# Reordering the start of a recurrent-attention and expert kernel: score copies, early loads and group preparation take other places in the queues

## The chip, the cores and the metric

One core of a Trainium2 chip runs the whole program. The metric is device time in microseconds, from the start to the end of one execution. A second number, the span, runs from the first to the last instruction that the profiler recorded on the core; the profiled execution has both. The engines are TensorE (PE; PEld is its weight load), VectorE (DVE), ScalarE (ACT), GpSimd (POOL) and SyncE (SP, which here only issues DMAs; SPq is its queue). Every engine takes its instructions strictly in the order in which the program lists them.

## What is computed

The reference is a recurrent attention over 768 steps, for 4 x 8 heads of width 40, whose output goes through a top-2 mixture of 8 experts:

```python
for t in range(S):
    y[:, :, t] = np.einsum('bhd,bhde->bhe', rt, state)
    Sa = np.einsum('bhde,bhe->bhd', state, at)
    state_decay = state * wt[:, :, None, :] - np.einsum('bhd,bhe->bhde', Sa, bt)
    state = state_decay + np.einsum('bhd,bhe->bhde', vt, kt)
...
logits = x @ w_gate                    # x: the attention output, 3072 x 320
noisy_logits = logits + np.log1p(np.exp(x @ w_noise)) * noise
# top 2 experts of each row, softmax of their two logits
h = np.maximum(x[mask] @ w1[e], 0.0)
out[mask] += top2_w[mask, k, None] * (h @ w2[e])
```

## The kernel before, in words

The attention is computed in chunks of 64 steps. The 4 batches are two pairs (p = 0, 1) and the 12 chunks are six groups of two (g = 0 to 5), so that each group has four blocks and the loop in `run` goes over 24 blocks n (g = n // 4; inside a group the chunk changes every two blocks and the pair every block). What a block needs of its group is prepared beforehand:

- `loadA` (L528) loads w (`raww`, two buffers) and b and a (`rawba`, one buffer; for group 0's second pair two `X` buffers instead). `prepA` (L536) makes the running product of w with a scan on VectorE (`Gx`), its reciprocal with a logarithm and an exponential on ScalarE (L546, L547), four products on VectorE (L549 to L554), multiplies b and a, and splits each into two 16-bit halves with `pack` (L495): ScalarE makes one half (L500), VectorE the other (L501). Six DMAs from SyncE's queue then stack the halves into `st_ab` (L568).
- `scoresL` (L602) multiplies the stacks on TensorE (`score32`) and ScalarE copies each result into `X` and `lo` (L609).
- With both pairs' scores in `X`, `cover` (L613) masks them, `turn` (L614) transposes them in 32 x 32 squares on VectorE, `tsolve` (L617) inverts with 30 steps of two products (on VectorE for group 0, on GpSimd for groups 1 to 5), and `turn` transposes back. `prepM`, `prepT` and `prepU` in `run` call these for a group: the mask, the first `turn` with the inverse, and the second `turn`.
- `loadC` and `prepC` (L582, L586) load the keys (`rawk`, one buffer), multiply and pack them, and write them to DRAM (`d_k`), from where `fetchA` reads them back as `st_k`. `fetchA` and `fetchR` (L628, L638) also load `Vz`, `vu` and `RV` for a block.

A block n then runs `pre` (its key scores), `blocks`, `chain` (TensorE applies the inverse, in `pQ`, and VectorE writes the state `Sst`, L730, kept as `s.aD`), `outp` (the block's output) and the router's `logits`. Inside the loop a block prepares pieces of the group two ahead.

What sets the order: the program is written down in one sequence, and a planner in the build then simulates it and gives each engine the instruction that is ready first by its own cost estimates; the written order breaks ties. Three means bind it: `issue_after(ins)` (named `after` in `run`) puts what a block of code creates on the engine of `ins` behind `ins`, on that engine alone; `Behind(tc, eng, first)` does so for each instruction called through it, on the engine `eng`; `high_priority` moves work ahead among what is ready. None of the three makes an engine wait for data.

Instructions called through `Behind` are recorded under its line, L436, those of `burst` and the matmul helpers under L511 and L512.

Once attention is over, the eight experts are computed (`experts`), each by two large matrix products, the first waiting for weights that are loaded where attention's buffers were.

Of the kernel before, what the change touches and what calls it, by code (L numbers as in the profile page):

```python
# [8 lines left out]
F32 = mybir.dt.float32  # L9
# [33 lines left out]
class Moe:  # L43
# [70 lines left out]
    def turn(s):  # L114

        s.early=s.decode("0",1,4)
# [324 lines left out]
class Att:  # L441
# [53 lines left out]
    def pack(s,src,scl,h,nc_,out,V=None):  # L495

        nc=s.nc
        pk=s.tmp.tile([120,nc_*2,X//nc_],F16,name="pk",bufs=PKB)
        v=pk.rearrange("p (c l) x->p c l x",l=2); sv=src.rearrange("p (c x)->p c x",c=nc_)
        nc.scalar.activation(v[:,:,h],sv,AF.Copy,scale=scl)  # L500
        s.pd=(V or nc.vector).scalar_tensor_tensor(v[:,:,1-h],sv,scl,v[:,:,h],op0=ALU.mult,op1=ALU.subtract)  # L501
        out(pk)
# [83 lines left out]
    def prepC(s,G,gate=None,kf=None,first=None):  # L586
# [5 lines left out]
        if p==0 and g==0:  # L592
            s.mags=s.cp.tile([120,1],F32,name="mags")
            nc.vector.tensor_reduce(s.mags,kf[:,0:64],axis=AX.X,op=ALU.max)
        k_=kf.rearrange("p (c a b t)->p c a (b t)",c=CG,a=3,b=2)
# [17 lines left out]
    def cover(s,Xt,eng): eng.tensor_tensor(Xt,Xt,s.tri.to_broadcast([128,32,32]),op=ALU.mult)  # L613
    def turn(s,Xt):  # L614

        v=Xt.rearrange("p a b->p b a"); return s.nc.vector.transpose(v,v)
    def tsolve(s,Xt,eng):  # L617
# [114 lines left out]
    def outp(s,o,sD,xout):  # L732
# [19 lines left out]
        xout=xout[:,0:DM]  # L752
        xo=xout.rearrange("p (h e)->p h e",h=8); nc.vector.tensor_tensor(xo,Y[:,:,0:40],xo,op=ALU.mult)

    def run(s,m,xo=None):
# [3 lines left out]
        def prepA(g,p):  # L759
            if p==0: grp[g]=[]; scr[g]=s.tmp.tile([128,32,32],F32,name="X",bufs=3)  # L760
            with s.tc.high_priority(offset=PA_):
                G=s.prepA(p,g,rA.pop((g,p),None),first.get((g,p))); grp[g].append(G); s.scoresL(G,p,scr[g])
        E=lambda g: nc.gpsimd if g in TPOOL else nc.vector
        def prepM(g): s.cover(scr[g],E(g) if g>1 else nc.vector)
        def prepT(g):
          with s.tc.high_priority(offset=PT_ if g else BURST):
            s.xd=s.turn(scr[g]); s.tsolve(scr[g],E(g))
        def prepU(g):
          with s.tc.high_priority(offset=PT_ if g else BURST):
            s.turn(scr[g]); scr2[g]=scr[g]  # L770
        def prepC(g,p): s.prepC(grp[g][p])
# [12 lines left out]
        rA[0,0]=s.loadA(0,0); rA[0,1]=s.loadA(1,0); kf=s.loadC({'p':0,'g':0})  # L784
        prepA(0,0); prepA(0,1); s.consts1()
        s.prepC(grp[0][0],kf=kf,first=s.pd); fA(0); fR(0)
        s.prepC(grp[0][1],first=s.pd); fA(1); fR(1)
        prepM(0); prepT(0); tl0=s.tl; tl=tl0.ins
        s.pre(O[0],s.tm); s.blocks(O[0])
        prepU(0)  # L790
        for n in range(4): fB(n)
        first[1,0]=first[1,1]=tl0
        prepA(1,0); prepA(1,1); prepM(1); prepT(1)
        if m is not None:
            with after(tl): m.consts2(s.dm.bitcast(F32))
        xts=[]; aD=tl0
        for n in range(N):
# [3 lines left out]
            if q%2==0 and gn<NG:  # L801
# [3 lines left out]
                grp[gn].append(s.prepA(q//2,gn,rA.pop((gn,q//2)),aD))  # L805
            if n<2: s.prepC(grp[1][n],first=tl0)
            elif q%2==0 and gn<NG:
                with behind(n-1): rC[gn,q//2]=s.loadC(grp[gn][q//2])
# [9 lines left out]
            aD=s.aD  # L818
            if q==2 and w+1<NG:
                prepU(w+1)  # L820
                for t in range(4): fB(4*w+4+t)
            if n+1<N: s.pre(O[n+1])
            if q==3 and gn<NG: prepT(gn)
            xt=s.wk.tile([128,360],F32,name="xt",bufs=2)
            s.outp(O[n],sD,xt); xt=xt[:,0:DM]
# [163 lines left out]
```

## Time and profile before

| what | value |
|---|---|
| timed runs, median of 3 | 975.82 us (973.9 to 977.76) |
| profiled execution | 969.27 us |
| its span | 967.4 us |
| busy in the span: PE, DVE, ACT, POOL | 763.3, 595.3, 382.3, 366.4 us |
| first use of an inverse by TensorE | 76.80 us |
| attention ends, experts follow | about 536 us |

A row of the timeline gives the start and the duration in us, the engine, the line, the operation, what it writes and reads with the shapes, how often it stands there in a row, and in brackets the idle time of the engine before it and what ended that. A DMA's row is its issue, not its landing. A row of the table by stretch gives for each engine the busy time and the number of instructions, then the granted TensorE clock as a share of its full rate, the DMA engines' busy share and GB/s. Averages over the span hide that its start, its loop and the experts have different limits, so the rows below are taken by stretch.

### The profile page before, as it was taken

The numbers are of one execution on the slowest core, as the hardware profiler recorded it, in microseconds if no ns is written. First come the engines' busy times: TensorE is split into PE (matmuls) and PEld (weight loads), VectorE is DVE, ScalarE is ACT, GpSimd is POOL, SyncE is SP. The second block draws the span as 40 slices with busy tenths as digits, with TensorE's granted clock in tenths as the row PEclk, the third lists the DMA queues.
The fourth block names the chain that finished last, engine by engine and source line by source line (L and its number), as shares of the span: only waits on it lengthen the run. The fifth ranks groups of instructions, "written<-read, shape, count | busy, mean of one in ns | idle before, by whom it ended". The sixth has DMA issues, their size and how long they took to land.

```text
span 967.4 us, 32608 instructions
## 1 busy us (share of the span) xinstructions
PE 763.3 (79%) x14248; PEld 675.4 (70%) x14248; DVE 595.3 (62%) x1295; ACT 382.3 (40%) x787; POOL 366.4 (38%) x516
## 2 busy tenths in 40 slices
PE   0115546898886878887999579899999999999994
PEld 0114435777775766766777478889899999998994
DVE  6499673767888697537657672673637372737340
ACT  3204342644533455333454432443434343434320
POOL 6000087087188049429300205224243525252312
PEclk9995557987977999888999799899999999999997
DMA  9524555475572645543331714556556656664412
GB/s 227 168 73 122 159 157 137 126 178 143 144 201 67 161 134 149 161 125 126 89 104 42 232 49 71 85 168 85 171 84 183 105 157 119 145 130 125 55 16 35
DMA packets 99507, 121.09 MB, mean 125 GB/s; under 512 B 37832, under 2 KB 83596, under 8 KB 99276
## 3 DMA queue, kind: packets, MB, share of 16 engines
q1 hardware_dynamic: 89244, 101.87, 39.9%
q0 software_dynamic: 10112, 17.05, 10.5%
q8 instruction: 114, 1.87, 0.9%
q14 instruction: 37, 0.30, 0.1%
HBM read 76.69 MB, written 24.74 MB: 105 GB/s over the span
## 4 chain that ended last, share of the span: by engine, by line
PE 48%; DVE 7%; POOL 4%; issue 3%; ACT 2%; another core or an unknown queue 2%; DMA 1%; SPq 0%; POOLq 0%; ACTq 0%
PE ph L303 18%; PE po L330 17%; PE psc L511 2%; POOL X L626 2%; POOL Tt L624 2%; PE pY L511 2%; PE pW L511 2%; PE pQ L511 1%; DMA w2r<-in_w_dram 1%; PE po L322 1%; PE po L320 1%; DVE ohB L165 1%; PE pst L511 1%; DVE ohA L163 1%
## 5 line engine op out<-in xcount | busy, mean ns | idle before, releaser
L333 POOL DMA_INDIRECT out_dram<-y,oi x56 | 88.7, 1583 | 203.7 <-ACT y L332 195.3
L303 PE MATMUL ph<-xT,w1h 128*128 128x256 f16 (+1 forms) x1280 | 141.8, 256 | 9.1 <-issue 4.9
L303 PEld LDWEIGHTS <-w1h 128*128 128x128 f16 x1280 | 110.4, 99 | 20.8 <-issue 12.3
L305 ACT ACTIVATE r<-ph 128x320 f32<-128x320 f32 (+1 forms) x128 | 65.4, 518 | 112.9 <-PE ph L303 66.1
L330 PEld LDWEIGHTS <-hh 128*128 128x128 f16 x1536 | 108.9, 98 | 0.8 <-issue 0.8
L626 POOL TENSOR_TENSOR X<-X,Tt 128x30 f32<-128x30 f32 (+9 forms) x150 | 96.3, 642 | 11.0
L303 PE MATMUL ph<-xT,w1l 128*128 128x256 f16 (+1 forms) x768 | 93.2, 256 | 6.2 <-issue 6.1
L624 POOL TENSOR_TENSOR Tt<-X 128x30 f32<-128x30 f32 (+9 forms) x150 | 92.4, 616 | 10.7
L241 DVE SCALAR_TENSOR_TENSOR w2l<-w2r,w2h 128x1280 f16<-128x1280 f32 x16 | 23.3, 1490 | 89.1 <-ACT w2h L240 88.0
L303 PEld LDWEIGHTS <-w1l 128*128 128x128 f16 x768 | 66.7, 99 | 12.9 <-issue 8.5
L307 DVE CAST hh<-r 128x320 f16<-128x320 f32 (+1 forms) x128 | 48.3, 378 | 44.2 <-ACT r L305 28.4
L259 POOL DMA_INDIRECT xr<-xd,gi x56 | 57.2, 1022 | 44.9 <-issue 14.3
L309 DVE TENSOR_TENSOR hl<-r,hh 128x256 f16<-128x256 f32 (+1 forms) x128 | 71.8, 561 | 3.9
L511 PE MATMUL psc<-RV,uT 128*64 128x128 f32 x384 | 61.7, 312 | 10.4 <-DVE P L743 7.0
L743 DVE TENSOR_TENSOR P<-psc,mk 128x512 f32<-128x512 f32 x48 | 33.0, 687 | 53.1 <-PE psc L511 53.0
L330 PE MATMUL po<-w2h,hh 128*128 128x160 f16 x768 | 62.2, 235 | 0.5 <-DVE tab L169 0.5
L511 PE MATMUL psc<-RV 128*64 128x128 f32 x384 | 61.7, 312 | 0.0
L511 PEld LDWEIGHTS psc<-RV,uT 128*64 128x64 f32 x384 | 48.3, 156 | 18.5 <-DVE P L743 9.3
L330 PE MATMUL po<-w2h,hl 128*128 128x160 f16 x768 | 61.1, 233 | 0.0
L330 PE MATMUL po<-w2l,hh 128*128 128x160 f16 x768 | 61.0, 233 | 0.0
L511 PEld LDWEIGHTS <-st_ab 120*32 120x32 f16 (+2 forms) x1312 | 26.7, 112 | 43.7 <-issue 38.5
L330 PEld LDWEIGHTS <-hl 128*128 128x128 f16 x768 | 54.7, 98 | 0.0
(321 smaller groups left out, 1577.0 us busy)
## 6 DMA issues: line engine op xcount, KB each, us to landing
st_ab<-pk SPq DMA_DIRECT2D x72, 180.0 KB
w2r<-in_w_dram SPq DMA_DIRECT2D x8, 1280.0 KB
RV<-in_rv_dram SPq DMA_DIRECT2D x48, 192.0 KB
w1r<-in_w_dram SPq DMA_DIRECT2D x8, 1024.0 KB
rawba<-in_fm_dram SPq DMA_DIRECT2D x22, 360.0 KB
raww<-in_fm_dram SPq DMA_DIRECT2D x12, 365.6 KB
rawk<-in_fm_dram SPq DMA_DIRECT2D x12, 360.0 KB
d_k<-pk SPq DMA_DIRECT2D x12, 360.0 KB
```

Of the source, the lines that this page charges most:

```text
L241: nc.vector.scalar_tensor_tensor(l,w,sc,o,op0=ALU.mult,op1=ALU.subtract,accum_out=s.wsum[:,s.nw:s.nw+1]); s.nw+=1
L259: k=t//128; s.held(nc.gpsimd.indirect_dma_start(out=X[:p,k if s.cap==CAP else 0],out_offset=None,in_=s.xd[int(w is not s.early[0])],in_off ...
L303: for a,b in cut(n): nc.tensor.matmul(ph[:,a:b],w[:,k,fs],X[:,j,t0+a:t0+b],start=i+a==0,stop=i==7,skip_group_check=True)
L305: g=nc.scalar.activation(r[:,:n],ph[:,:n],AF.Relu,scale=HSC/(XS*W1S))
L307: nc.vector.tensor_copy(hh[:,f,:n],r[:,:n])
L309: if c.stop>c.start: nc.vector.tensor_tensor(o,r[:,c],hh[:,f,c],op=ALU.subtract)
L330: for a,b in cut(DM): s.lm=nc.tensor.matmul(po[:p,a:b],h[:,f,r],w[:,f,a:b],start=k+a==0,stop=k==23,skip_group_check=True)
L333: st=nc.gpsimd.indirect_dma_start(out=s.out_d,out_offset=OFFS(ap=idx[:p,e,ii:ii+1],axis=0),in_=y[:p],in_offset=None,compute_op=ALU.add)
L511: def mm(s,*a,**k): return lambda: s.nc.tensor.matmul(*a,**k)
L624: eng.tensor_tensor(t,Xt[:,j:j+1,j+1:].to_broadcast([128,j,m]),Xt[:,0:j,j:j+1].to_broadcast([128,j,m]),op=ALU.mult)
L626: s.tl=eng.tensor_tensor(Xt[:,0:j,j+1:],Xt[:,0:j,j+1:],t,op=ALU.add)
L743: nc.vector.tensor_tensor(m,pp.rearrange("p i j t->p (i j) t"),s.mk.to_broadcast([128,8,64]),op=ALU.mult)
```

## The change

The score copies, the loads and the preparation of group 1 get other places; no arithmetic is changed.

- `scoresL` of both pairs of group 0 is written after both preparations, and its ScalarE copies stand behind `s.pa`, ScalarE's last pack of the second pair.
- The small constant copies `consts1` come first. The maximum over the keys (`mags`) goes through `V`, so it stands behind the second pair's last pack on VectorE.
- `sd` is the last stack DMA of the second pair. The loads of blocks 0 and 1 (`fA`, `fR`), the key work's DMAs of pair 1, and the router's loads (`consts2`) stand behind it on SyncE's queue.
- The load of group 1's first pair is written before `prepA(0,1)`; its preparation `prepA(1,0)` is written before the mask of group 0 and stands behind the key pack of pair 0, and the mask stands behind its last pack.
- `pre` and `blocks` of block 0 stand behind the last score copy on ScalarE.
- `tb` is the second transpose of group 0. The key work of pair 1, `prepA(1,1)`, the mask of group 1 and the key work of group 1 stand behind it. Group 2's first preparation stands behind the first transpose of group 1 (`aD=s.xd`).
- The second transpose of later groups (`prepU`) is written further down in the block and stands behind the block's state update `s.aD`; for group 1 it moves from the third block (q = 2) to the fourth (q = 3).
- `high_priority` with an offset of 0 is taken off `prepA`.

```diff
-        nc.scalar.activation(v[:,:,h],sv,AF.Copy,scale=scl)
+        s.pa=nc.scalar.activation(v[:,:,h],sv,AF.Copy,scale=scl)
...
-            nc.vector.tensor_reduce(s.mags,kf[:,0:64],axis=AX.X,op=ALU.max)
+            V.tensor_reduce(s.mags,kf[:,0:64],axis=AX.X,op=ALU.max)
...
-    def turn(s,Xt):
+    def turn(s,Xt,f=None):
-        v=Xt.rearrange("p a b->p b a"); return s.nc.vector.transpose(v,v)
+        v=Xt.rearrange("p a b->p b a"); return (Behind(s.tc,s.nc.vector,f) if f is not None else s.nc.vector).transpose(v,v)
...
         def prepA(g,p):
             if p==0: grp[g]=[]; scr[g]=s.tmp.tile([128,32,32],F32,name="X",bufs=3)
-            with s.tc.high_priority(offset=PA_):
-                G=s.prepA(p,g,rA.pop((g,p),None),first.get((g,p))); grp[g].append(G); s.scoresL(G,p,scr[g])
+            grp[g].append(s.prepA(p,g,rA.pop((g,p),None),first.get((g,p))))
+        def scores(g,p): s.scoresL(grp[g][p],p,scr[g])
         E=lambda g: nc.gpsimd if g in TPOOL else nc.vector
-        def prepM(g): s.cover(scr[g],E(g) if g>1 else nc.vector)
+        def prepM(g,f=None): s.cover(scr[g],E(g) if g>1 else Behind(s.tc,nc.vector,f))
...
-        def prepU(g):
+        def prepU(g,f=None):
           with s.tc.high_priority(offset=PT_ if g else BURST):
-            s.turn(scr[g]); scr2[g]=scr[g]
+            s.tb=s.turn(scr[g],f); scr2[g]=scr[g]
...
         rA[0,0]=s.loadA(0,0); rA[0,1]=s.loadA(1,0); kf=s.loadC({'p':0,'g':0})
-        prepA(0,0); prepA(0,1); s.consts1()
-        s.prepC(grp[0][0],kf=kf,first=s.pd); fA(0); fR(0)
-        s.prepC(grp[0][1],first=s.pd); fA(1); fR(1)
-        prepM(0); prepT(0); tl0=s.tl; tl=tl0.ins
-        s.pre(O[0],s.tm); s.blocks(O[0])
-        prepU(0)
+        s.consts1()
+        prepA(0,0); rA[1,0]=s.loadA(0,1); prepA(0,1); sd,pd=s.sd0.ins,s.pd
+        with after(s.pa.ins):
+            for p in range(2): scores(0,p)
+        s.prepC(grp[0][0],kf=kf,first=pd)
+        with after(sd): fA(0); fR(0)
+        first[1,0]=s.pd; prepA(1,0)
+        prepM(0,s.pd); prepT(0); tl0=s.tl; s.tm0=s.tm
+        with after(s.sl.ins): s.pre(O[0],s.tm); s.blocks(O[0])
+        prepU(0); tb=s.tb
         for n in range(4): fB(n)
-        first[1,0]=first[1,1]=tl0
-        prepA(1,0); prepA(1,1); prepM(1); prepT(1)
+        with after(sd):
+            s.prepC(grp[0][1],first=tb); fA(1); fR(1)
+        first[1,1]=tb
+        prepA(1,1); scores(1,0); scores(1,1); prepM(1,tb); prepT(1)
         if m is not None:
-            with after(tl): m.consts2(s.dm.bitcast(F32))
-        xts=[]; aD=tl0
+            with after(tb.ins),after(sd): m.consts2(s.dm.bitcast(F32))
+        xts=[]; aD=s.xd
...
-            if n<2: s.prepC(grp[1][n],first=tl0)
+            if n<2: s.prepC(grp[1][n],first=tb)
...
-            if q==2 and w+1<NG:
-                prepU(w+1)
-                for t in range(4): fB(4*w+4+t)
             if n+1<N: s.pre(O[n+1])
             if q==3 and gn<NG: prepT(gn)
+            if q==(2 if w else 3) and w+1<NG:
+                prepU(w+1,s.aD)
+                for t in range(4): fB(4*w+4+t)
```

## Rows read from the trace of the kernel before

**Rows 1.** Busy time by stretch: us, then PE, PEld, DVE, ACT, POOL.

```profile
76.80:178.30 101.50, 61.22 (x1409) 50.63 (x1411) 66.50 (x91) 38.13 (x79) 38.68 (x61) 0.64 0.57 152
...
536.30:967.40 431.10, 388.37 (x4780) 364.76 (x4778) 217.77 (x557) 160.45 (x274) 146.13 (x115) 0.95 0.53 113
```

**Rows 2.** Timeline of DVE, first 50 us: start, duration, line, operation, idle before.

```profile
4.80 1.78 DVE L543 TENSOR_TENSOR_SCAN Gx<-raww,d 120x780 f32<-120x780 f32 x1 [0.90 <-DMA raww<-in_fm_dram]
8.37 0.96 DVE L549 TENSOR_TENSOR NH<-Gx,raww 120x768 f32<-120x768 f32 x1 [1.79 <-ACT raww L547]
...
13.36 0.22 DVE L594 TENSOR_REDUCE mags<-rawk 120x1 f32<-120x64 f32 x1 [0.98 <-DMA rawk<-in_fm_dram]
...
16.25 1.78 DVE L543 TENSOR_TENSOR_SCAN Gx<-raww,d 120x780 f32<-120x780 f32 x1
17.94 0.93 DVE L501 SCALAR_TENSOR_TENSOR pk<-rawba,pk 120x768 f16<-120x768 f32 x1
...
22.34 0.96 DVE L549 TENSOR_TENSOR NH<-Gx,raww 120x768 f32<-120x768 f32 x1 [3.38 <-ACT raww L547]
...
32.09 1.83 DVE L501 SCALAR_TENSOR_TENSOR pk<-X,pk 120x768 f16<-120x768 f32 x2 [4.02 <-ACT pk L500]
...
35.77 0.96 DVE L436 SCALAR_TENSOR_TENSOR pk<-rawk,pk 120x768 f16<-120x768 f32 x1 [0.82 <-ACT pk L500]
44.94 1.03 DVE L436 TENSOR_TENSOR rawk<-rawk,NH 120x384 f32<-120x384 f32 x2 [8.21 <-DMA rawk<-in_fm_dram]
45.92 1.23 DVE L613 TENSOR_TENSOR X<-X,tri 128x1024 f32<-128x1024 f32 x1
```

**Rows 3.** Timeline of ACT, first 50 us.

```profile
20.46 0.24 ACT L60 ACTIVATE wg<-wgn 128x48 f16<-128x48 f32 x1 [4.27 <-DMA wgn<-in_wgn_dram]
...
30.67 0.38 ACT L609 ACTIVATE X<-psc 128x256 f32<-128x256 f32 x1 [8.36 <-PE psc L511]
```

**Rows 4.** Timeline of SyncE's queue, first 50 us: issues of DMAs.

```profile
19.88 5.10 SPq L568 DMA_DIRECT2D st_ab<-pk  x6
25.03 0.96 SPq L534 DMA_DIRECT2D rawba<-in_fm_dram  x2
...
32.09 4.97 SPq L568 DMA_DIRECT2D st_ab<-pk  x6
```

**Rows 5.** Timeline of PE: first use of group 0's inverse.

```profile
76.80 1.29 PE L511 MATMUL pQ<-w,X 32*32 32x40 f32 x64 [8.37 <-DVE nge L436]
```

**Rows 6.** Timeline of DVE: the inverse of group 0 and its second transpose.

```profile
50.00 0.15 DVE L624 TENSOR_TENSOR Tt<-X 128x30 f32<-128x30 f32 x1
...
72.63 0.21 DVE L626 TENSOR_TENSOR X<-X,Tt 128x30 f32<-128x30 f32 x1
...
74.61 2.05 DVE L616 STREAM_TRANSPOSE X<-X 128x1024 f32<-128x1024 f32 x1
```

**Rows 7.** Timeline of DVE, blocks 1 to 3.

```profile
111.06 0.96 DVE L436 TENSOR_TENSOR rawba<-rawba,NH 120x768 f32<-120x768 f32 x1 [5.03 <-DMA rawba<-in_fm_dram]
...
126.39 1.31 DVE L436 TENSOR_TENSOR rawk<-rawk,NH 120x384 f32<-120x384 f32 x2 [5.11 <-DMA rawk<-in_fm_dram]
...
164.53 1.99 DVE L616 STREAM_TRANSPOSE X<-X 128x1024 f32<-128x1024 f32 x1 [7.61 <-POOL X L626]
...
178.34 0.49 DVE L730 SCALAR_TENSOR_TENSOR Sst<-pS,gam 128x320 f32<-128x320 f32 x1 [0.68 <-PE pd L512]
```

**Rows 8.** Timeline of POOL: start of group 1's inverse, and a step inside it.

```profile
121.20 0.15 POOL L619 MEMSET X<- 128x32 f32 x1 [103.14 <-DVE X L616]
...
147.09 0.62 POOL L624 TENSOR_TENSOR Tt<-X 128x240 f32<-128x240 f32 x1
```

**Rows 9.** Timeline of DVE: one product, alone and beside GpSimd.

```profile
88.32 0.96 DVE L436 TENSOR_TENSOR NH<-Gx,raww 120x768 f32<-120x768 f32 x1 [0.33 <-ACT raww L547]
...
131.64 1.28 DVE L436 TENSOR_TENSOR NH<-Gx,raww 120x768 f32<-120x768 f32 x1
```

**Rows 10.** Waits of DVE from 178.3 to 536.3: total us, times, longest.

```profile
DVE X L616 <- POOL X L626: 6.3, 3, 3.5
```

More of the change, by code (lines that the diff above doesn't have):

```diff
@@ L752, in outp @@
         xout=xout[:,0:DM]
-        xo=xout.rearrange("p (h e)->p h e",h=8); nc.vector.tensor_tensor(xo,Y[:,:,0:40],xo,op=ALU.mult)
+        xo=xout.rearrange("p (h e)->p h e",h=8); s.xo=nc.vector.tensor_tensor(xo,Y[:,:,0:40],xo,op=ALU.mult)
     def run(s,m,xo=None):
```

## The prediction

> **What bounds the kernel now.** I first split the span at the end of the attention part. After 536.3 us TensorE is busy 388 of 431 us [rows 1]; that part computes the experts, nothing in it is edited, and it starts when attention ends, so I count it as fixed. The change must show before that. The second look is VectorE's order of work (DVE) in the first 50 us, reading only the idle times and who ended them [rows 2]; the third is ScalarE (ACT) and SyncE at the same times [rows 3, 4]. The chain to the first attention block is: pack both pairs of group 0, stack them by DMA, 32-wide scores, copies by ACT, the mask ("cover"), a transpose, the 30-step inverse on DVE, a second transpose, and TensorE's first use of the inverse at 76.80 [rows 2, 5, 6]. The fourth look is the stretch from there to the fourth block's state update, 178.34 [rows 7]: four blocks take 101.5 us, in which DVE works 66.5 and idles 35.0 [rows 1].
>
> The reader should see three faults at the start. ACT waits 4.27 us for the router weights (wgn) before it does the logarithm of the second pair, and DVE waits 3.38 us for that [rows 2, 3]. ACT's score copies of the first pair wait 8.36 us for TensorE while the second pair's packs stand behind them, and DVE waits 4.02 us [rows 2, 3]. And DVE then idles 8.21 us before the key products of the second pair, with the mask right behind them [rows 2], while group 1 is not yet prepared.
>
> **The change part by part.** Up to the second pair's last pack. The key maximum moves behind that pack: its 0.98 us wait goes [rows 2]. The router loads move behind the second pair's stacks on SyncE, and with them ACT's wait; what is left is the time of logarithm and exponential, 1.79 us after a scan as in the first pair [rows 2]. The second scan ends at 18.03, so the next step could start at 19.82, while DVE is busy to 18.87: 0.9 us of wait instead of 3.38, a gain of 2.5. With the copies queued behind the packs the 4.02 goes; ACT's first pack fits beside DVE's next product. Together 0.98 + 2.5 + 4.0 = 7.5: the last pack ends at 26.4 instead of 33.9 [rows 2].
>
> What is late next: the scores of the second pair. Before, 12.0 us pass from its last pack (33.92) to the mask (45.92) [rows 2], with two loads of group 1 (rawba) just ahead of the six stack transfers on SyncE's queue [rows 4]. The new order still issues that rawba load ahead of them, but Vz, vu, RV, wgn, nz and the zeros for xd stand behind them now. At the old 12.0 us the scores are ready at 38.4, and this is the upper bound I need.
>
> That wait is filled on purpose: key products of pair 0 (1.03 + 0.82 wait + 0.96 = 2.8 [rows 2]) and the whole preparation of group 1, pair 0. Its price is that of group 0's first pair: from 4.80 to 18.87, 14.07, less the 0.98 wait, 0.2 of key maximum and 1.7 of the other pair's scan: 11.2, or 12.1 if the scan no longer covers one ACT pack [rows 2]. 26.4 + 2.8 + 12.1 = 41.3, later than the scores, so the mask waits for DVE's own queue, not for data. The transpose follows and the inverse starts 3.2 us after the mask (4.1 before, with a 0.9 us key pack between) [rows 2, 6]: 44.5 instead of 50.0. It lasts 22.8 to 72.84; then 1.8 us of group 1 stood ahead of the second transpose (2.05) [rows 6], which the change frees of them: 44.5 + 22.8 + 2.1 + 0.15 = 69.5 for TensorE's first use, against 76.80 [rows 5]: **7.3 us**. Bounds: 9 if ACT's packs stay covered; 3 if ACT's score copies stand ahead of group 1's logarithm and cost DVE a second 4.02.
>
> From there to the fourth state update. Of DVE's 66.5 us, group 1's first pair goes: 11.2 less its 1.8 of waits and the 1.8 scan already done by then, 7.6. Key products of pair 0's partner come in, 2.0 (they now stand behind the second transpose; the n=1 block needs them, but that block used the inverse only long after, so they are covered by block 0; uncovered they cost 2.8 plus a trip through DRAM). That leaves 60.9. Of the 35.0 idle, three waits should go: 5.03 for rawba, 5.11 for rawk, 7.61 for GpSimd at group 1's second transpose, which held the state update behind it [rows 7]. The two loads have single buffers and are released earlier by the earlier preparation; the transpose moves from the third block to behind the fourth block's state update. 17.3 are left, short waits on TensorE and ACT that I keep.
>
> Two costs come in. The mask of group 1 waits for its second pair's stacks with only key products and block work beside it: between 0 and 12.0 (the same path above), I take 5, since block work fills half. And group 1's inverse on GpSimd, which started at 121.20 after 103 us of nothing [rows 8], now starts near 102 (pack near 87, plus 12 to the mask, plus 3.3), so both preparations of group 2 run beside it: the same 768-wide product takes 0.96 alone and 1.28 beside GpSimd [rows 9], 9 such operations more, 3 us. The Trainium skill, "SBUF — State Buffer", section "Who interferes with whom", says that a VectorE operation with two SBUF inputs and a GpSimd operation that reads SBUF lock each other out for a whole instruction. By that rule the sum would lose up to one GpSimd operation, 0.62 [rows 8], at each of the 9, an estimate of 5.6 us instead of 3; the rows bear out that both sides wait, at the smaller price.
>
> Sum: 69.5 + 60.9 + 17.3 + 5 + 3 = 155.7 against 178.34, **22.6 us**. GpSimd's inverse, 43 us long [rows 7, 8], ends near 145 and is not late. After this point the loop has the same work per block; its second transposes now stand behind the block's state update in every group. They waited 6.3 us for GpSimd in all, three times [rows 10]; I count that at 0, bounds from a gain of 2 each to a loss below. The other edits only return handles.
>
> **The rivals.** (a) Deeper: TensorE's and ACT's short waits shrink too, since blocks 1 to 3 stop standing in queues behind stalled preparation. 8 of the 17.3 and the 5 go: the update at 143. Then GpSimd's end at 145 holds the transpose, so 35 us is the most. For: TensorE is busy only 61 of the 101.5 us [rows 1].
> (b) Only the start counts: blocks 1 to 3 are paced by group 2's preparation in the order fixed at build time, and the removed waits come back at other loads. Only 7 or 8 us. For: single buffers for rawba and rawk remain. Against: a whole preparation has left that stretch.
> (c) It doesn't do what it says: the edges fix order on one engine only, and another load or copy holds the first mask at 45.9 or later, while the freed DVE time later falls into waits. No change.
> (d) Slower: the second transposes of groups 2 to 5. DVE serves its queue in order, and a transpose that waits for GpSimd also holds the score masks and the next state update. If four of them wait as group 1's did, 7.61 each [rows 7], 30 us are paid against 22.6: 8 slower. It decides the sign above 5.7 each. Against: before, three such waits sum to only 6.3 [rows 10], and the transposes move later, not earlier.
>
> **How the numbers follow.** The profiled execution took 969.27 us (span 967.4); the timed runs have a median of 975.82, 6.55 more. Off the profiled time the forecast is 946.7; on the scale of the timed runs 975.82 - 22.6 = 953. Rival (a) 941, (b) 968, (c) 976, (d) 983. Chances: forecast 0.58, (a) 0.14, (b) 0.14, (c) 0.05, (d) 0.09. The terms' own bounds (first use 3 to 9 us early; mask wait 0 to 12) give the forecast 944 to 964; the range reaches to (a) and (b) with a little room, 937 to 971, and leaves out (c) and (d). About 0.5% (5 us) is what a measurement of this kernel can tell from no change. Faster: forecast, (a) and most of (b), 0.83; same: (c) and the rest of (b), 0.08; slower 0.09.
>
> **What would show it.** DVE's last pack of the second pair near 26 without the 3.38 and 4.02 waits; group 1's scan ahead of the first mask; the inverse from about 44; TensorE's first use near 69; no 5 us DMA waits for rawba and rawk around blocks 1 and 2; GpSimd's first inverse near 102; the fourth state update near 156, and all later blocks ahead by the same amount. I am wrong if that lead shrinks between the fourth update and the end of attention, or if the mask waits for the second pair's stacks beyond 41, or if DVE waits over 5 us for GpSimd at several transposes.

## The result, and the profile after

| what | before | after |
|---|---|---|
| timed runs, median | 976.71 us (973.9 to 977.76, 4 runs) | 964.41 us (962.4 to 970.21, 4 runs) |
| ratio, 95% interval | | 0.9888 [0.9839, 0.9938] |
| profiled execution, its span | 969.27, 967.4 us | 962.40, 960.6 us |
| first use of an inverse | 76.80 | 75.37 |
| fourth state update | 178.34 | 172.81 |
| attention ends | 536.3 | 522.3 |
| from there to the end | 431.1 | 438.3 |

The change makes the kernel 12 us faster, by the interval 6 to 16 us. The forecast was 22.6 us (953 us). A second comparison of the two, later, gave 0.9822 [0.9777, 0.9866], which is 17 us (954.9 against 971.77), and a second profile of each; where two numbers stand for one kernel below, they are these two executions. The ratios, and the time of 947.58 us below, leave out executions that fell in a slower state. The profiles show less than the timed runs: the profiled executions of the two kernels differ by 6.9 and 5.9 us, because both of the kernel before ran 7 and 11 us under its timed median. Where the timed runs have the rest is not shown. To follow the blocks I use ScalarE's copy `Ut`, of which each of the 24 blocks has one; attention's end is that of the last.

Busy time by stretch of the kernel after, the first stretch of [rows 1] (us, then PE, PEld, DVE, ACT, POOL, granted clock, DMA share, GB/s):

```profile
75.37:172.81 97.44, 59.14 (x1413) 49.18 (x1415) 62.62 (x85) 37.72 (x78) 46.83 (x61) 0.75 0.58 152
```

DVE works 62.6 us there and idles 97.4 - 62.6 = 34.8, as much as before (35.0). The granted TensorE clock is 0.75, before it was 0.64 [rows 1]; PE's busy time fell by 2.1 us with it, little beside the 38 us that PE idles there.

Timeline of DVE in the kernel after, the start, answering [rows 2] and [rows 6]:

```profile
18.64 0.96 DVE L549 TENSOR_TENSOR NH<-Gx,raww 120x768 f32<-120x768 f32 x1 [0.85 <-ACT raww L547]
...
24.32 1.83 DVE L501 SCALAR_TENSOR_TENSOR pk<-X,pk 120x768 f16<-120x768 f32 x2
...
29.08 1.78 DVE L436 TENSOR_TENSOR_SCAN Gx<-raww,d 120x780 f32<-120x780 f32 x1
...
45.69 0.96 DVE L436 SCALAR_TENSOR_TENSOR pk<-rawba,pk 120x768 f16<-120x768 f32 x1 [7.32 <-ACT pk L500]
...
47.52 1.22 DVE L436 TENSOR_TENSOR X<-X,tri 128x1024 f32<-128x1024 f32 x1
...
50.82 0.15 DVE L624 TENSOR_TENSOR Tt<-X 128x30 f32<-128x30 f32 x1
```

The old waits are gone as forecast: 3.38 became 0.85, the 4.02 before the last packs is 0, and these end at 26.15; the scan of group 1 stands ahead of the mask. But DVE now waits 7.32 us for an ACT pack of group 1's first pair, and the mask behind that pack comes at 47.52, later than before (45.92); the inverse starts at 50.82, not at 44.5 as forecast. Timelines of ACT and of PE, same kernel, same place:

```profile
42.71 1.76 ACT L514 ACTIVATE kb<-ptr 64x320 f32<-64x320 f32 x4 [4.61 <-PE ptr L511]
44.67 0.24 ACT L60 ACTIVATE wg<-wgn 128x48 f16<-128x48 f32 x1 [0.20 <-DMA wgn<-in_wgn_dram]
44.82 1.57 ACT L500 ACTIVATE pk<-rawba 120x768 f16<-120x768 f32 x2
```

```profile
41.49 0.64 PE L511 MATMUL psc<-st_ab,st_k 120*64 120x64 f16 x16 [4.10 <-DMA st_k<-d_k]
...
75.37 1.29 PE L511 MATMUL pQ<-w,X 32*32 32x40 f32 x64 [6.65 <-DVE X L616]
```

ACT stands before block 0's key copies (kb), which need the keys' trip through DRAM (st_k from d_k, 4.10 us of wait on PE), and then copies the router's weights; the packs that DVE needs are third in its queue.

Timeline of DVE, blocks 1 to 3, answering [rows 7] and [rows 9]:

```profile
106.02 1.23 DVE L436 TENSOR_TENSOR X<-X,tri 128x1024 f32<-128x1024 f32 x1 [5.16 <-ACT X L609]
...
109.87 1.74 DVE L436 TENSOR_TENSOR_SCAN Gx<-raww,d 120x780 f32<-120x780 f32 x1
...
121.24 2.05 DVE L436 TENSOR_TENSOR_SCAN Gx<-raww,d 120x780 f32<-120x780 f32 x1
...
131.24 1.43 DVE L436 TENSOR_TENSOR rawk<-rawk,NH 120x384 f32<-120x384 f32 x2 [2.10 <-DMA rawk<-in_fm_dram]
132.71 1.28 DVE L436 TENSOR_TENSOR NH<-Gx,raww 120x768 f32<-120x768 f32 x1
...
136.51 0.68 DVE L743 TENSOR_TENSOR P<-psc,mk 128x512 f32<-128x512 f32 x1
...
143.94 0.68 DVE L743 TENSOR_TENSOR P<-psc,mk 128x512 f32<-128x512 f32 x1
...
165.15 0.69 DVE L743 TENSOR_TENSOR P<-psc,mk 128x512 f32<-128x512 f32 x1 [4.80 <-PE psc L511]
...
172.81 0.49 DVE L730 SCALAR_TENSOR_TENSOR Sst<-pS,gam 128x320 f32<-128x320 f32 x1 [0.69 <-PE pd L512]
```

The waits for rawba (5.03) and for GpSimd at the second transpose (7.61) are gone. What stands in their place is read from the waits of DVE in this stretch (75.37 to 172.81; total us, times, longest):

```profile
DVE P L743 <- PE psc L511: 10.8, 4, 4.8
DVE X L436 <- ACT X L609: 5.2, 1, 5.2
DVE rawk L436 <- DMA rawk<-in_fm_dram: 4.4, 3, 2.1
DVE ak L665 <- PE psc L511: 4.2, 1, 4.2
```

In DVE's timeline above, both scans of group 2 (109.87, 121.24) with their products stand in the queue ahead of block 1's two products `P`. PE in the same stretch shows who waits for those, and a stall of 3.74 us that the trace puts to no other engine, only to `issue`:

```profile
144.67 1.94 PE L511 MATMUL pY<-kb,P 128*64 128x64 f32 x32 [4.66 <-DVE P L743]
...
147.19 1.29 PE L511 MATMUL pQ<-w,X 32*32 32x40 f32 x64
...
159.96 0.65 PE L511 MATMUL pY<-sD,RV 128*64 128x40 f32 x7 [3.74 <-issue]
```

Block 2's first use of the inverse (147.19) stands behind block 1's `pY`, and that behind DVE's `P`. GpSimd's part, answering [rows 8]: group 1's inverse runs from 110.19 to 161.56, 51.4 us, which took 43 before.

```profile
110.10 0.16 POOL L619 MEMSET X<- 128x32 f32 x1 [91.62 <-DVE X L616]
```

And the waits of DVE for GpSimd at later second transposes, answering [rows 10]: 4.6 us in two, where there were 6.3 in three (second profiles: 6.4 in two, 7.1 in three).

```profile
DVE X L436 <- POOL X L626: 4.6, 2, 2.9
```

### The profile page after: what moved, and what is told of

Read it like the earlier page. It is cut to its first block, busy times and chain, and to the rows that moved or that the text cites. A ratio compares the mean times of both kernels' runs of the same rounds, so it can differ in the third digit from the quotient of the medians.

```text
span 960.6 us, 32605 instructions
## 1 busy us (share of the span) xinstructions
PE 759.0 (79%) x14248; PEld 670.7 (70%) x14248; DVE 597.5 (62%) x1295; ACT 381.5 (40%) x787; POOL 374.2 (39%) x516
## 3 DMA queue, kind: packets, MB, share of 16 engines
q0 software_dynamic: 10112, 17.05, 10.6%
## 4 chain that ended last, share of the span: by engine, by line
PE 58%; DVE 21%; issue 7%; DMA 5%; ACT 3%; another core or an unknown queue 2%; SPq 1%; POOL 0%; DVEq 0%; POOLq 0%; ACTq 0%
PE ph L303 18%; PE po L330 17%; PE psc L511 4%; PE pY L511 4%; PE pW L511 3%; PE pQ L511 2%; DVE pk L436 2%; PE pS L511 2%; DVE Gx L436 2%; DVE rawba L436 1%; DVE X L616 1%; DMA w2r<-in_w_dram 1%; DVE ohB L165 1%; PE pst L511 1%
## 5 line engine op out<-in xcount | busy, mean ns | idle before, releaser
L626 POOL TENSOR_TENSOR X<-X,Tt 128x30 f32<-128x30 f32 (+9 forms) x150 | 100.6, 671 | 11.0
L624 POOL TENSOR_TENSOR Tt<-X 128x30 f32<-128x30 f32 (+9 forms) x150 | 96.2, 641 | 10.7
L259 POOL DMA_INDIRECT xr<-xd,gi x56 | 56.2, 1003 | 44.5 <-issue 14.3
L332 ACT ACTIVATE y<-po,tab 128x320 f32<-128x320 f32 x44 | 22.9, 521 | 79.1 <-PE po L330 79.1
```

What stands on the lines that cost most here:

```text
L259: k=t//128; s.held(nc.gpsimd.indirect_dma_start(out=X[:p,k if s.cap==CAP else 0],out_offset=None,in_=s.xd[int(w is not s.early[0])],in_off ...
L624: eng.tensor_tensor(t,Xt[:,j:j+1,j+1:].to_broadcast([128,j,m]),Xt[:,0:j,j:j+1].to_broadcast([128,j,m]),op=ALU.mult)
L626: s.tl=eng.tensor_tensor(Xt[:,0:j,j+1:],Xt[:,0:j,j+1:],t,op=ALU.add)
```

## The experiments

My theory after seeing the two traces: the start brought nearly nothing, since ACT's queue put block 0's copies ahead of the packs; and what the kernel gained comes from the second transposes, which no longer make DVE wait for GpSimd. Rivals: GpSimd's inverse beside DVE ate the gain; or the preparation of group 2 was moved the wrong way; or attention gained it all and the experts gave it back. Each edit is against the changed kernel unless it says otherwise; each ratio is against the kernel before on the same chip, since that kernel's median lay between 970.82 and 980.57 in the four comparisons.

**Block 0's copies behind the packs.** `pa1` is ACT's last pack of group 1's first pair; the lines that these replace are left out.

```diff
+        first[1,0]=s.pd; prepA(1,0); pa1=s.pa.ins
...
+        with after(s.sl.ins),after(pa1): s.pre(O[0],s.tm); s.blocks(O[0])
...
+            with after(tb.ins),after(sd),after(pa1): m.consts2(s.dm.bitcast(F32))
```

> The changed kernel with one edit: ScalarE's copies for block 0 (kb) and the router's weight copy stand behind the last pack of group 1's first pair. Theory A (these copies, which wait for the keys' trip through DRAM, hold the pack and so the mask): VectorE's 7.3 us wait before that pack goes, the mask starts near 41.5 instead of 47.5 and TensorE first uses the inverse near 69.5 instead of 75.4. If blocks 1 to 3 follow the start, the fourth state update comes near 167 instead of 172.8 and the time falls by 6 us to about 958. Rival B (blocks 1 to 3 are paced by the preparation of group 2 in VectorE's order): first use near 69.5 too, but the fourth update within 2 us of 172.8 and the time within 3 us of 964. Rival C (the scores' own DMA holds the mask): mask still at 46 or later, nothing moves.

Measured 957.2 us against 970.82, 0.9845 [0.9803, 0.9888]. The first use came at 69.8, the fourth update at 164.3. Run again beside the changed kernel:

> The kernel with block 0's copies and the router copy held behind group 1's packs, once more, now beside the changed kernel on one chip. If the start counts as the first profile showed (fourth update at 164.3 against 172.8), it is 4 to 8 us faster than the changed kernel, ratio near 0.982; if the loop gives the lead back each time (364.0 then against 351.5), it equals the changed kernel within 2 us. The stall of 4.54 us before TensorE's router product at 314 should shrink to about 1 us if it changes from run to run, and stay if it belongs to the order.

947.58 us against 971.77, 0.9729 [0.9663, 0.9795], the changed kernel there 954.9: 7.3 us faster than it, and the fastest seen. The earlier comparison, without the changed kernel beside it, had 13.6 us against before, hardly more than the 12 of the changed kernel. Timelines of DVE, ACT and PE in the second run:

```profile
38.34 1.83 DVE L436 SCALAR_TENSOR_TENSOR pk<-rawba,pk 120x768 f16<-120x768 f32 x2
40.09 1.22 DVE L436 TENSOR_TENSOR X<-X,tri 128x1024 f32<-128x1024 f32 x1
...
165.08 0.48 DVE L730 SCALAR_TENSOR_TENSOR Sst<-pS,gam 128x320 f32<-128x320 f32 x1
```

```profile
37.47 1.71 ACT L500 ACTIVATE pk<-rawba 120x768 f16<-120x768 f32 x2 [1.59 <-DVE rawba L436]
42.15 1.76 ACT L514 ACTIVATE kb<-ptr 64x320 f32<-64x320 f32 x4 [2.97 <-PE ptr L511]
```

```profile
70.03 1.29 PE L511 MATMUL pQ<-w,X 32*32 32x40 f32 x64 [6.66 <-DVE X L616]
```

With the two orders swapped on ACT the 7.32 is gone, the mask comes at 40.09 and the first use at 70.0, where the prediction had 41.3 and 69.5; the fourth update comes at 165.1. So ACT's order was the step that failed, and the price of the start came out. It did so with two small misses that cancel: the mask is 1.2 us early, and behind it DVE waits 2.02 us for a small product of TensorE (`gam<-pg`), which the prediction did not have.

**The second transposes back in their old place.** The changed kernel with this part undone:

```diff
+            if q==2 and w+1<NG:
+                prepU(w+1)
+                for t in range(4): fB(4*w+4+t)
-            if q==(2 if w else 3) and w+1<NG:
-                prepU(w+1,s.aD)
-                for t in range(4): fB(4*w+4+t)
```

> The changed kernel with one part undone: the second transposes of groups 1 to 5 are written where they were before (third block, ahead of the next block's key scores, tied to nothing). Theory A (the 8.5 us by which the lead grows between the fourth block and the end of attention comes from these places): the lead at the end of attention falls from 14 to about 5 us, the end comes near 530 instead of 522.3, and the time rises by 8 us to about 972. Rival B (that growth comes from the other edits, through the planner's new order): the end stays within 2 us of 522 and the time within 3 us of 964.

Measured 967.78 against 970.82, 0.9973 [0.9951, 0.9994]: hardly faster than before. Its timeline of DVE shows what holds block 2's state update:

```profile
162.21 1.97 DVE L616 STREAM_TRANSPOSE X<-X 128x1024 f32<-128x1024 f32 x1 [9.02 <-POOL X L626]
```

The work moved at the start shows as a longer wait for GpSimd (9.02, before 7.61); the fourth update is at 179.7. The expectation had sought this gain in the loop and the end of attention near 530; the lead is gone by block 2 already, and attention ends at 538.9.

**The second transposes alone.** The kernel before with only this part of the change (and the argument `f` of `turn` that it needs):

```diff
-            if q==2 and w+1<NG:
-                prepU(w+1)
-                for t in range(4): fB(4*w+4+t)
+            if q==(2 if w else 3) and w+1<NG:
+                prepU(w+1,s.aD)
+                for t in range(4): fB(4*w+4+t)
```

> The kernel before with one part of the change alone: the second transposes of groups 1 to 5 stand behind the block's state update and behind the next block's key scores, group 1's in the fourth block. Theory A (most of the gain comes from this part: VectorE no longer waits for GpSimd ahead of block 2's state update, and the start edits bring next to nothing, as with the transposes put back): fourth state update near 170 instead of 178.3, ratio to the kernel before 0.990. Rival B (the parts need each other: the start edits bring the lead, the transposes only keep it): fourth update within 3 us of 178, ratio 0.997 or above.

971.51 against 980.57, 0.9906 [0.9866, 0.9945], about 9 us: most of what the whole change brings. The waits of DVE for GpSimd, in the kernel before (its second profile, all of the span) and in this one:

```profile
DVE X L616 <- POOL X L626: 15.6, 4, 8.5
```

```profile
DVE X L436 <- POOL X L626: 5.2, 2, 3.5
```

10.4 us of waits go (8.7 against the first profile of before, 13.9). The fourth update comes at 171.1, the changed kernel's at 172.8 and 170.9: the same within what two executions differ. With this edit in place the rest of the change adds nothing by then; from there to the end of attention the changed kernel is 6 us ahead (522.3 and 521.9 against 528.4).

**Group 1's inverse left out.** 28 of the 30 steps of group 1's inverse are left out, so GpSimd works 3.6 us there instead of 51.

```diff
+        for j in (range(20,31,10) if short else range(1,31)):
...
+            s.xd=s.turn(scr[g]); s.tsolve(scr[g],E(g),g==1)
```

> The changed kernel with 28 of the 30 steps of group 1's inverse left out on GpSimd, so group 1's attention is not the reference's. Theory A (GpSimd's inverse, which now runs beside both preparations of group 2, stretches VectorE's products from 0.95 to 1.2 to 1.5 us and so blocks 1 to 3): products at 0.95 again, the fourth state update 5 to 8 us earlier than 172.8. Rival B (the order in VectorE's queue paces these blocks, whatever the length of its products): the products are short again, yet block 2's first use of the inverse stays within 3 us of 147.2 and the fourth update within 3 us of 172.8.

One execution, 954.67. Timeline of DVE, the product that takes 1.28 at 132.71 in the changed kernel:

```profile
134.59 0.96 DVE L436 TENSOR_TENSOR NH<-Gx,raww 120x768 f32<-120x768 f32 x1
```

The price of one product is confirmed. From first use to fourth update it takes 169.3 - 76.6 = 92.7 us, with the inverse 97.4 and 96.5: GpSimd's company costs at most 4 to 5 us in blocks 1 to 3, where the prediction had 3. At most, because TensorE's `issue` stalls are 2 us shorter here as well (5.2 us in three, against 7.3 in two). Block 2 hardly moves (`Ut` 152.4 against 153.5). So this rival explains a small part. The Trainium skill, "SBUF — State Buffer", section "Who interferes with whom", would let each such instruction wait for up to a whole one of the other engine. Here a product grows by 0.32 us (1.28 against 0.96), about half of a GpSimd operation (0.62 [rows 8]), so the rule's full price is not reached; the measurement decides.

**Group 1's first preparation back behind the second transpose of group 0.**

```diff
-        first[1,0]=s.pd; prepA(1,0)
...
-        first[1,1]=tb
-        prepA(1,1); scores(1,0); scores(1,1); prepM(1,tb); prepT(1)
+        first[1,0]=first[1,1]=tb
+        prepA(1,0); prepA(1,1); scores(1,0); scores(1,1); prepM(1,tb); prepT(1)
```

> The changed kernel with one edge moved: the preparation of group 1's first pair stands behind group 0's second transpose again, so nothing stands ahead of group 0's mask but its scores. Theory A (as the prediction priced it: the preparation fits into the wait for the scores, so moving it out gains little at the start and costs its 10 us of VectorE time later): mask near 38.5, first use of the inverse near 66.5, but mask of group 1 near 112 or later instead of 106 and the fourth state update 3 to 8 us later than 172.8; ratio 0.993. Rival B (what counts is the first use, blocks 1 to 3 follow it): fourth update near 164, ratio 0.982.

968.68 against 980.57, 0.9867 [0.9792, 0.9942]: by this interval not shown to differ from the changed kernel (0.9888 and 0.9822). Timelines of DVE and of PE:

```profile
36.93 1.23 DVE L436 TENSOR_TENSOR X<-X,tri 128x1024 f32<-128x1024 f32 x1 [7.96 <-ACT X L609]
```

```profile
64.81 1.29 PE L511 MATMUL pQ<-w,X 32*32 32x40 f32 x64 [6.66 <-DVE X L616]
```

With nothing to fill it the wait for the scores is 7.96 us, but the first use comes at 64.8, 10.6 us ahead of the changed kernel; the preparation then fills blocks 0 to 2, and the fourth update is at 175.4. What is gained at one end is paid at the other: the fourth update speaks for theory A (2.6 us later than 172.8), the ratio lies between the two.

**The order of group 2's preparations.** Two edits, the first preparation earlier (behind group 0's second transpose) and the second later (behind the last product of block 1's output, `s.xo`):

```diff
-        xts=[]; aD=s.xd
+        xts=[]; aD=tb
```

> The changed kernel with one edge moved: the preparation of group 2's first pair stands behind group 0's second transpose instead of behind group 1's first one, so VectorE may do it while it waits for the scores of group 1 (some 12.6 us idle between 91 and 106). Theory A (group 2's two preparations, both between block 1 and block 2, hold block 2): block 2's first use of the inverse falls from 147.2 to about 137, the fourth state update to about 164, time 956. Rival B (what is late is GpSimd's or TensorE's own work): block 2 within 3 us of 147, time within 3 us of 964. Rival C: the preparation now stands ahead of group 1's mask and waits for its own load; mask of group 1 at 112 or later instead of 106, GpSimd's inverse ends past 168, time 965 to 970.

```diff
-                grp[gn].append(s.prepA(q//2,gn,rA.pop((gn,q//2)),aD))
+                grp[gn].append(s.prepA(q//2,gn,rA.pop((gn,q//2)),s.xo if n==2 else aD))
```

> The changed kernel with one edge moved: the preparation of group 2's second pair stands behind the output of block 1 instead of behind the state update of block 1. Theory A (VectorE's order holds block 2: the score masks of block 1's output stand behind that preparation): block 2's first use of the inverse falls from 147.2 to about 137, its end from 153.5 to about 143; the preparation itself ends about as much later, and the fourth state update falls by 3 to 8 us from 172.8. Rival B (GpSimd's stretch of VectorE's products, or TensorE's own queue, holds block 2): within 3 us of 147.2. On the sum of both: time 957 to 962 for A on the scale where the changed kernel has 964.

Earlier: 963.86 against 970.82, 0.9930 [0.991, 0.9949]. It only exchanges waits, as its timeline of DVE shows; the mask of group 1 slips to 121.2, the fourth update is 4 us earlier (168.7), attention ends 6 us later (528.5), and the time is not better.

```profile
117.73 1.03 DVE L436 TENSOR_TENSOR rawk<-rawk,NH 120x384 f32<-120x384 f32 x2 [10.14 <-DMA rawk<-in_fm_dram]
```

Later: 980.7 against 980.57, 0.9993 [0.9957, 1.0029], the whole gain lost. Timelines of PE and DVE:

```profile
140.92 0.79 PE L511 MATMUL pQ<-w,X 32*32 32x40 f32 x64
```

```profile
133.99 1.44 DVE L436 TENSOR_TENSOR rawk<-rawk,NH 120x384 f32<-120x384 f32 x2 [5.53 <-DMA rawk<-in_fm_dram]
...
143.30 1.57 DVE L436 TENSOR_TENSOR rawk<-rawk,NH 120x384 f32<-120x384 f32 x2 [4.50 <-DMA rawk<-in_fm_dram]
```

This is a miss for my reading of blocks 1 and 2. The order of the queue did hold block 2: its first use of the inverse comes 6.3 us earlier (140.92 against 147.19). But DVE now stands 5.53 and 4.50 us before the loads of the one key buffer, which the preparation had covered; block 2's `Ut` comes only at 152.4, PE also waits 3.64 for ACT between, and the fourth update is at 175.0, 2 us later instead of 3 to 8 earlier. The two combined with the first experiment:

> Both edits on the changed kernel: block 0's ScalarE copies behind the packs, and the second preparation of group 2 behind the output of block 1. If both mechanisms hold and add up: first use of the inverse near 69.8, fourth state update near 160 (164.3 with the first edit alone), ratio to the kernel before 0.980. If GpSimd's inverses have become the limit: first use the same, but VectorE waits over 5 us for GpSimd at the second transposes of groups 1 and 2, and the ratio stays at 0.984 to 0.986 as with the first edit alone.

976.67 against 980.57, 0.9957 [0.9923, 0.9992]; first use 71.0, fourth update 171.1, against 164.3 without the later preparation. Neither of the two cases came: the ratio is above both, and the waits for GpSimd are 6.4 us in all, one of them over 5.

> The same with group 2's first preparation held behind group 0's second transpose instead of group 1's first, so that it stands ahead of group 1's mask and the P products of block 1 come earlier. From the two edits by themselves (fourth update 164.3 and 168.7, against 172.8): 160 if they add, 164 if both take the same wait. Mask of group 1 near 115. Ratio 0.980 if they add and the loop keeps it; 0.985 or more if not.

952.14 against 971.77, 0.9796 [0.9742, 0.985]; fourth update 164.0, the case in which both take the same wait; on the same chip the first edit alone has 0.9729. The edits don't add. A second key buffer, which would separate load and order, wasn't tried.

**The same kernels again.**

> The kernel before once more, unedited, for a second profile beside the next three. Theory N (the experts part, 431 us in one profile of before and 438 in that of after, differs from execution to execution and not by the edit): its experts part lies anywhere from 428 to 440 us, its fourth state update again within 1 us of 178.3, and the loop from the fourth block to the last within 3 us of 360. Rival: 431 within 1 us each time, so that the 7 us more in after belong to the edit.

> The changed kernel once more, unedited. Theory N: first use of the inverse 75.4 and fourth state update 172.8 again within 1 us, since no long transfer decides there; the loop, 351.5 us in the first profile against 360.0 before, comes back between 351 and 364, so that its 8.5 us are not a gain of the order; experts 428 to 440. Rival: loop 351.5 again within 2 us, which would make the shorter loop a property of the order that the planner wrote. Ratio near 0.989.

The time in us by stretch of `Ut`, each kernel's two executions:

| stretch | before | after | block 0 behind the packs |
|---|---|---|---|
| start to block 3 | 176.3, 175.3 | 170.8, 168.9 | 161.7, 161.3 |
| block 3 to 7 | 70.5, 71.9 | 72.6, 72.7 | 76.7, 76.8 |
| block 7 to 11 | 86.5, 87.7 | 80.0, 78.4 | 86.8, 80.2 |
| block 11 to 23 | 203.1, 197.7 | 198.9, 201.9 | 200.4, 197.5 |
| experts | 431.1, 426.6 | 438.3, 431.4 | 431.5, 429.8 |

The start repeats within 2 us. Means of before and after: -5.9 in the start, +1.5 in blocks 4 to 7, -7.9 in blocks 8 to 11, 0 behind, -12.3 in attention; the experts have +6, so that -6.3 is left of the whole. That the -12.3 equal the timed 12 us is chance. The experts go with the chip: 428.2 to 432.2 us in the four profiles of one chip, 436.5 to 440.5 in the four of another, 426.6 to 431.4 in the four of a third, whichever kernel ran. So the 7 us more in one profile of after are no cost shown to be the change's. The mended kernel (last column) leads the changed one by 9.0 and 7.6 us at block 3 and gives back 4.1 of them in blocks 4 to 7, both times.

The second profile of after also answers its expectation: the loop took 353.0 us after 351.5, which both theories allowed, but before had 360.0 and 357.2, so it was shorter both times; the fourth update, 170.9, lies outside the 1 us expected. Blocks 8 to 11 repeat for before and after, and DVE's timeline shows one reason: the kernel before (second profile), and after (second profile).

```profile
311.87 2.02 DVE L616 STREAM_TRANSPOSE X<-X 128x1024 f32<-128x1024 f32 x1 [2.41 <-POOL X L626]
313.93 0.49 DVE L721 TENSOR_SCALAR vu<-pQ 64x320 f32<-64x320 f32 x1
```

```profile
301.50 0.49 DVE L721 TENSOR_SCALAR vu<-pQ 64x320 f32<-64x320 f32 x1
...
308.37 0.48 DVE L730 SCALAR_TENSOR_TENSOR Sst<-pS,gam 128x320 f32<-128x320 f32 x1
308.77 2.06 DVE L436 STREAM_TRANSPOSE X<-X 128x1024 f32<-128x1024 f32 x1
```

Before, block 10's `vu` stands behind the transpose that waits for GpSimd. After, `vu` and the update come first, and GpSimd has ended (307.9) when the transpose's turn comes. Update to update, block 10 takes 27.0 us before (295.04 to 322.02) and 19.0 after (289.36 to 308.37); in the first profiles it took 24.0 and 18.4. The wait and the transpose are 4.4 of the 8.0; the rest goes with the order of group 4's preparation, in which `P` now stands ahead of the last products (argued from the rows, not tested by itself). With the transposes alone block 10 takes 23.5 us, with all but the transposes 21.4, so both parts have a share. A rival stands untested: over blocks 8 to 11 the granted clock rose from 0.84 and 0.82 to 0.89 and 0.91, and PE's busy time fell from 68.1 and 68.9 us to 61.8 and 61.0, with some 35 of 1669 matmuls moved behind block 11. Whether the clock made these blocks shorter or the denser work raised the clock, no run separates.

## Why the prediction was partly wrong

**The start, 7.3 us: measured 1.4 and 2.6.** Up to the packs it held (26.15 against 26.4). The step that failed is "the mask waits for DVE's own queue, not for data". I had bounded a copy on ACT ahead of group 1's logarithm, but at 4 us and for the score copies; it was block 0's key copies, waiting for a trip of the keys through DRAM, at 7.32. With that order mended the start came out at 69.8 and 70.0, as priced.

**Blocks 1 to 3, 15.3 us: measured 4.1** (101.5 to 97.4; 3.8 in the second profiles). DVE's work was nearly right, 62.6 against 60.9 + 3, and GpSimd's price (3, at most 4 to 5 measured), though its inverse began at 110 and not near 102. The term that was mis-sized is the idle time: three waits of 17.75 us were to go, leaving 17.3 + 5 = 22.3, and 34.8 stayed. Of the 12.5 us between, 4.4 are the rest of the wait for rawk, 0.2 the mask's, and 7.9 came into the "short waits on TensorE and ACT that I keep": 34.8 - 4.4 - 5.2 = 25.2 instead of 17.3. The one before `P` alone is 10.8, in the profile of before 5.5.

Two things stand behind that, and how they share the 7.9 is not shown. One is a term that the prediction put at nothing: TensorE's `issue` stalls, rows of which stand in the last section. In this stretch they are 3.61 and 3.74 us in one execution, 4.62 and 2.65 in the other. The longest wait before `P` follows the second stall: 4.80 and 3.78. The mask's wait follows the first: 5.16 - 3.61 and 6.17 - 4.62 are both 1.55 us, and four other kernels that stall there have the same rest within 0.01 (the two remaining profiles 1.10 and 1.70). So the 5 us priced for the second pair's stacks were met by luck. The kernel before has one such stall here (3.07), which reaches DVE by way of ACT as a wait of 1.66 us; the transposes alone have none over 1 us, and there the stretch takes 93.0 us. The other thing is the order that rival (b) describes, of `P`, preparation and key loads: the two edits of group 2's order show a removed wait replaced by the next one. But a lead at the start is not lost here: with ACT's order mended, 5.6 and 4.4 us at the first use are 8.5 and 5.9 at the fourth update. And (b) is wrong in its other half, that the start's 7 or 8 us remain.

**The loop, 0 us: measured about -6.** I bounded the later transposes by a gain of 2 each from their waits alone [rows 10]. What stands behind a waiting transpose counts more than the wait: block 10 got 5.6 and 8.0 us shorter, while the waits themselves only went from 6.3 and 7.1 to 4.6 and 6.4. How much of this is the granted clock's stays open. Rival (d) had the right queue and the wrong sign, since the move behind the update gives GpSimd more time.

**The transposes as such.** I counted the 7.61 as one of three waits among many. The two experiments on this part give it about 9 us alone, and the rest of the change 3 alone; together that is the first comparison's 12, and 5 short of the second's 17. With ACT's order mended there would have been 7.3 us more. That the mended kernel ends 24.2 us under before, near the 22.6 of the forecast, is in part chance: its other comparison had 13.6, only 12 to 14 us stand at the fourth update, where the forecast had 22.6, and the rest comes behind, where the forecast had nothing.

## What to carry to other kernels

When an instruction is moved to fill a wait, follow it on every engine that it uses: here the place of its two ACT packs cost 7.32 us, more than was left of the gain at the start. A wait by an in-order engine for a slow helper is cheapest behind the recurrence's own update; count what is queued behind it, not its length. In a stretch whose engines each idle a third or more, removed waits need not add up: 17.75 us of them were to go here, and the stretch got 4.1 us shorter. And split a wait into what precedes it on the engine waited for before calling its price confirmed: the mask's 5.16 us were 3.61 us of something else.

## What the hardware showed beside

TensorE has stalls that the trace puts to no wait, only to `issue`. One stands in the same group of matmuls in eight of the profiles, with a varying length. Three executions' timelines of PE: the changed kernel twice, and the kernel with block 0 behind the packs (second time).

```profile
104.00 1.01 PE L511 MATMUL pW<-q,lo 32*32 32x40 f32 x24 [3.61 <-issue]
```

```profile
103.79 1.01 PE L511 MATMUL pW<-q,lo 32*32 32x40 f32 x24 [4.62 <-issue]
```

```profile
98.66 1.01 PE L511 MATMUL pW<-q,lo 32*32 32x40 f32 x24 [2.02 <-issue]
```

The second execution of the changed kernel has a second stall at the same place as the first execution's 3.74 above (PE), and the two waits of DVE that follow the stalls, the mask and `P`:

```profile
159.32 0.43 PE L511 MATMUL pY<-sD,RV 128*64 128x40 f32 x7 [2.65 <-issue]
```

```profile
105.82 1.23 DVE L436 TENSOR_TENSOR X<-X,tri 128x1024 f32<-128x1024 f32 x1 [6.17 <-ACT X L609]
...
163.55 0.69 DVE L743 TENSOR_TENSOR P<-psc,mk 128x512 f32<-128x512 f32 x1 [3.78 <-PE psc L511]
```

The mask's row names ACT, which copied the scores; the score products themselves stand right behind the stalled matmul on TensorE. Another stall, before a router product, took 4.54 in one execution of that last kernel and 0.44 in its next:

```profile
314.13 0.30 PE L104 MATMUL pl<-wg,xT 128*128 128x48 f16 x4 [4.54 <-issue]
```

```profile
308.95 0.26 PE L104 MATMUL pl<-wg,xT 128*128 128x48 f16 x4 [0.44 <-issue]
```

This is part of why blocks 7 to 11 took 86.8 and 80.2 us there. What the sequencer waits for is not shown by these rows, but the DMA records of the same traces point somewhere: of the 32 stalls over 1.5 us in attention, over all profiles, 28 end 1.27 to 1.73 us behind the end of a 16,384-byte transfer on the DMA queue that the profile calls `instruction` (114 such transfers in each execution). That suggests that TensorE waited for instructions; no run changed these transfers, so it is not shown.
